# One order of 2764 operations for another, in a four-layer attention kernel: where a stream of matmuls, three busy engines and a few queues set the pace

## The chip, the core and the metric

The kernel runs on one core of a Trainium2 chip. Five engines work side by side, each with its own queue of instructions that it takes strictly in order: TensorE (PE in the profile, with PEld for the loading of its weights), VectorE (DVE), ScalarE (ACT), GpSimd (POOL) and SyncE (SP), which here only starts transfers. Engines wait for each other through semaphores. The metric is the device time of one execution in microseconds.

## The reference

Four residual layers run on one sequence of 2048 tokens with 512 features: a linear-attention block (A), a sliding-window attention block (B), and both once more with the same weights. There are 32 heads of 16 features. Cut to what matters:

```python
def A(x, wqkv, wo):
    q, k, v = heads(x @ wqkv)
    phi = lambda t: jnp.where(t > 0, t + 1, jnp.exp(t)) + 1e-6
    pq, pk = phi(q), phi(k)
    kv, z = einsum("bhsd,bhse->bhde", pk, v), einsum("bhsd->bhd", pk)
    o = einsum("bhqd,bhde->bhqe", pq, kv) / (einsum("bhqd,bhd->bhq", pq, z)[..., None] + 1e-6)
    return merge(o) @ wo

def B(x, wqkv, wo):                       # W = 256
    q, k, v = heads(x @ wqkv)
    scores = einsum("bhqd,bhkd->bhqk", q, k) * 16 ** -0.5
    scores = where((0 <= i - j) & (i - j < W), scores, -1e9)
    return merge(einsum("bhqk,bhkd->bhqd", softmax(scores), v)) @ wo

x = x + A(layernorm(x)); x = x + B(layernorm(x))
x = x + A(layernorm(x)); x = x + B(layernorm(x))
```

## The kernel before

The sequence is cut into 16 tiles of 128 tokens. All four layers are recorded as 2764 operations (a list `s.ops`, built by `graph`), each with the engines that may run it, the buffers it reads and writes, and a function that emits its instructions. Names carry their layer: `1.` is the k and v side of the first linear layer, `2.` its q side and the second layer (the sliding window; `2.b` its projections, `2.a` its attention), `2k.` the k and v side of the third layer, `3.` the q side of the third and the whole fourth (`3.b`, `3.a`). Nothing of layer 3's k side needs more than the tile of its own rows, so layers overlap; but each linear layer's sum over all tokens must be complete before any of its q tiles is used, and this makes a narrow place near 45 us and another near 250 us.

The operations that the text speaks of, by their lines:

- `ln` (lines 814 to 820): mean and variance on DVE, 1/sqrt on POOL (`rs`, line 818), normalised rows `xn` on DVE (line 820). `transp` then turns `xn` into `xT`, either by a DMA transpose that SP starts (line 828) or, for a few tiles, by PE (line 835) and a copy.
- `proj_tok` (line 858): a projection with 128x512 results, four matmuls of 512 columns in two halves; `proj_feat` (line 870): sixteen matmuls of 128 columns. Weights are w_Aq, w_Ak, w_Av, w_Ao for the linear layers and w_Bq, w_Bk, w_Bv, w_Bo for the window layers.
- `phi` (lines 879 to 885): exponential and relu on ACT, the rest on DVE.
- `b_qkv`: two masked copies `kbd` of k per tile (`kb0`, `kb1`, line 971), a copy of q and one of v (line 845). Each of these may run on ACT or on DVE. POOL then starts four transfers that lay v out by heads (`vd`, line 981).
- `b_attn`: scores by four row groups (lines 1007 and 1056, 32 and 16 matmuls in an operation), exponentials on ACT over 128x1024 (lines 1035 and 1077), masks on DVE (lines 1043 and 1095), then the sums over keys with 34-column matmuls (lines 1113 and 1125), the division on DVE and the output projection.

What runs when is not decided when the program is built: a text `ORDER` holds one word for each operation, in order of planned time, and `schedule` walks through it. A word is the operation's number, a mark ' where the second of its possible engines is taken (for the copies the first is ACT, the second DVE), and after a colon the places of its new buffers (PSUM banks, ring slots). Each engine's queue is the words of that engine in this order; `emit` derives the waits from the reads and writes. The text was made beforehand by a planner that is not part of the kernel.

```python
for word in self.plan.split():
    word, _, at = word.partition(":")
    o = self.ops[int(word.rstrip("'"))]
    o.eng, cost = list(o.engs.items())[word.endswith("'")]
```

One more thing depends on the order. Where the half of a `proj_tok` is followed on PE by an operation of another mode, its last matmul is emitted as two, of 448 and 64 columns:

```python
cut = [0, 448, 512] if at[0].cut and kt % 2 else [0, 512]
```

The program also has a slow general path (`general`), taken only when a value is not finite; it isn't executed here.

PE's instructions on the executed path: every matmul is two (its weights, then the multiplication), and a wait that doesn't fit into a matmul is one of its own. Before, they add up to 17,048.

Of the kernel before, what the change touches and what calls it, by code (L numbers as in the profile page):

```python
# [334 lines left out]
230:5.0 194 299 231 184 224:4.0.0 200' 148 207:9 214:7.1 215 300 238:0 271:10 196 195 197 216 208:2.1.3 209 210 180 225 228 284 212 179 278:7.2 279 272:6.2.1  # L335
152 285 286:1 181 301 302:2 314 315 316 169 211 280' 255:11 226 227 229 273 317 213 318:3 256:3.3.2 257 274 239:12 232' 275 25 16 258 259 34 260 23 261 24
262:4.3 263 26 27 246:7.4 240:2.4.0 185 241 247 276 264' 287:13 244 288:5.5.3 201 289 303:14 290 291 310:6.5 311 312' 292 242 248 319:15 294:3.6 277 304:4.7.2
305 308 295 320:5.6.1 306 321 322 324 217 326:2.7 327 243 28 29 17 245 233 249 265 293 307 309 296' 281 297 313 323 328 325 329 330:0 331:1 378:7.4.0 379 380
# [9 lines left out]
658' 671 626 627 672 673 902:6 907:2 684 903 986:0.4.1 987 988 919 449:0 904 955 905:3 881:1 906:3 882:3 883 921:0.6.0 922 923 908 909 685 686:2 687:1 450:5  # L348
884 1407 960:3.0.3 451 961 910:2 911 677:2.1.5 678 912:2 989 962 1408 924 1409 452 474:6.0 475 476 488 477 478:2 479:3 937:3 938 679 933:0.4.1 934 935 674:2.1
675 700 701 1410 932 939 940:1 720 964:0.6.2 702 703 965 966 688:5.0 689 690 691 1411:3 936 942:4 1412:0 941:1 489:0.3 490 943 501 676' 1021:2.6.2 1022 944  # L350
1023 704:0 491 492 493:0 494:1 705:3 967 692:5.2 693 945:2 946 947:0 680 963 721 694' 956:0.2.0 957 958 954 480:4 481 482 644 645 662 1418:7.1 995:0.5.4 996
997 722:1 723:2 1419 1420' 990 913:4 914 915 968:0.2.5 969 970 495:7 496 713:6.2.0 714 715 959 503 497 504:0.0 505 999:4.2.1 1000 1001 972:7 971 977:6 506 973
507 508:3 1056:0.4.0 1057 1058 1024 736 737 974 975:1 738 976:2 978 979 991:0.2.0 992 980:3 981 1421 1422 1423 998 710:7.3 711 712' 993 706:6.1 707 708' 709'
1030:0.4.3 681 716 1031 1032 695:3.1.1 696 994 948:2 1002 1003:0.6.2 697' 1004 949 950 1435 509:3 982:2 510:5 983:4 984 1005 1006 663 1034:0.2.5 1035 985 1036
511 1012:7 512 772 1436 1437 739 1438 740:2 741:4 1060 1007:6 1008 1439:3 1440:2 1424 1449 1450 1091:0.4.1 1092 754 1093 513:3.12.1 514 515 1013 1014 1009
1010:2 1451 517 1011:0 1026:0.4.0 1027 1028 728:2.0 1015:0 1016 1413:3.1.0 1414 1415 729 755 1425:0 1426:1 698 1037 1065:0.6.1 1066 730' 1416 1417 1067
731:5.0.3 732 724:4.2 733 725 1038:0.2.2 1039 1040 1441:7.0.2 1446:6.0 1447 1442 1029 1025 1033 1042:5 1443 1069:0.2.4 1070 1071 726' 1095 1043 727'
1427:4.4.3 1428 1429 699 1452 1448' 1453:1 1041 1047:6 1044 1126:0.2.2 1127 756 1444 1445 1068 746:7.1 747 1017:1 1045:1 1454:5 1046:1 1128 1430 1431 1048
1094 1061:0.4.0 1062 1063 1049 748' 1050:3 1051 757 1052:0 758:2 759:0 1018:3 1019 1100:0.6.3 1101 1102 1020 1465 1466 1467 1460:2.4 773 774 1455:5.3.0 1456
1073:0.3.5 1103 1461 1074 1457 1462 1432:7.3 742:6.3 1433 743 1075 775 1072 1059 1064 1077:2 1078 744 1458 1459 1104:0.4.2 1105 1106 1076 1434' 1079 1082:3  # L360
1083 745' 1080:2 1081:3 516 717 1161:0.6.0 1162 1163 1084 1085:0 764:2.2 765 1086 518 1087:2 766' 1096:0.4.0 1097 1098 1130 749:3.1.2 750 767:2.2.4 776:3 1107
1165 1135:0.6.1 1136 751' 1137 768 769' 1053:5 777:3 1054 1108:0.3.4 1099 1055 1479 760:2.4 761 762' 1468 1109 1110 1111 734 1112:7 1139:0.5.5 1140 1141 1113
1114 763' 1115:1 770 1469:0 1117:4 1118 1116:2 752 1196:0.2.1 519:5.3 1129 520 1197 521 522 1198 523:0 524:3 1119 1120:2 543:7.13.2 544 545 1480 1121 547
1088:1 1199 1131:2.5.0 1142 1089 1090 782:4.3 783 1164 1493 1132 1133 1134 528:7.14.3 1138 1170:0.2.3 1171 784' 1172 529 530 532 778:6.5 779 780' 781' 525:5
526 1143:0.2.2 753 1144 1145 527 790 791 735 1147:4 1148 792 1122:1 1494 1149 1150:0 1146 1151:1 1174:0.6.4 1175 793 1176 794:1 546 1470:3 1476:5.2 1477
1471:3.2.0 1478' 1177 1472 1473 1474 1475 1152:4 1153 1231:0.6.2 1232 1233 1481 531 1482 1154 1155:1 1156 1123:5 533 1124 1166:0.2.0 1125 1507 1173 558:4.15.1
# [3 lines left out]
1484:4 1269 1504:4.6 1505 1204 812:0 1240:0.6.3 1241 1242 1158:2 1159 1502 1506' 1503 1510 1160 1523 1192:3 1524 1193:3 1194 1195 1537 807 1213:0.4.4 1214  # L370
813:2 1217:2 1215 1218 1219 1220:1 1221:2 1244:0.6.5 1245 1246 1485:3.7.1 549:4.3 1212 550 551 1538 552 553:3 554:1 1539 1216 1486 1487 1488 1489 818:2.1 819
820 814:1.1 1235 1236:4.6.0 1237 815 816' 1243 1238 821:0.2.0 822 823 1247 1239 1463:5.4 817 1275:2.6.1 1464 1222:0 1223 1224 1276 1277 1248:2.4.2 1249 1525
# [996 lines left out]
```

## Time and profile before

| what | value |
|---|---|
| time, median of 3 runs | 421.62 us (420.8 to 422.5) |
| time of the profiled execution | 422.47 us |
| span from its first to its last instruction | 421.1 us, granted clock 1.000 |
| PE busy | 392.3 us, 93% of the span |
| ACT busy | 383.6 us, 91% |
| DVE busy | 382.3 us, 91% |
| POOL busy | 106.0 us, 25% |
| moved by DMA | 29.22 MB in 75,720 packets |

The profile counts an engine as busy while an instruction of it runs; the chain that ended last follows, from the last instruction backwards, what released each step. "issue" is time in which an engine waited for nothing that the profile shows. An instruction's mean duration is longer than the step from one to the next, since they overlap in the engine: an exponential of 128x1024 has 1085 ns, and the chain has it six times in 5.50 us.

### The profile page before, as it was taken

What the parts mean: (1) busy time and instruction counts of PE and PEld (TensorE: products, weight loads), DVE (VectorE), ACT (ScalarE), POOL (GpSimd) and SP (SyncE); (2) the same over time, 40 slices, a digit from 0 to 9 for tenths busy, and PEclk for the clock granted to TensorE, in tenths of its full rate; (3) what the DMA queues carried; (4) which work ended last, traced back from release to release, by engine and by line L of the source; (5) the groups of instructions that cost most, each with busy time, mean ns of one, the idle gap of its engine ahead of it and who ended that gap; (6) DMA issues with size and microseconds to landing.
All of it is one profiled execution on the core that took longest, in us unless ns stands there. A gap on an engine that the chain in (4) does not pass through costs nothing.

```text
span 421.1 us, 18887 instructions
## 1 busy us (share of the span) xinstructions
PE 392.3 (93%) x8330; PEld 284.2 (67%) x8404; DVE 382.3 (91%) x1003; ACT 383.6 (91%) x496; POOL 106.0 (25%) x202
## 2 busy tenths in 40 slices
PE   7999989999999899998999999998999899988997
PEld 3655766776766676767586667676767667666675
DVE  7999899999999899998999899999999999978774
ACT  4888679999999999999899767899999999999995
POOL 2230024225232231423131100332322212605200
PEclk9999999999999999999999999999999999999999
DMA  8334426314252130523141201324415422406143
GB/s 265 112 64 138 128 55 126 66 41 99 41 68 43 38 67 16 85 41 59 39 80 22 48 9 39 70 48 68 79 34 80 60 52 33 90 16 117 43 103 92
DMA packets 75720, 29.22 MB, mean 69 GB/s; under 512 B 65264, under 2 KB 73584, under 8 KB 75632
## 3 DMA queue, kind: packets, MB, share of 16 engines
q1 hardware_dynamic: 70336, 22.36, 26.4%
q0 software_dynamic: 4096, 4.46, 5.7%
q8 instruction: 68, 1.11, 1.1%
q10 hardware_dynamic: 1200, 1.11, 0.9%
q14 instruction: 20, 0.16, 0.1%
HBM read 6.29 MB, written 2.10 MB: 20 GB/s over the span
## 4 chain that ended last, share of the span: by engine, by line
PE 42%; ACT 33%; DVE 18%; issue 3%; DMA 3%; POOL 0%; DVEq 0%
ACT pF L1077 23%; PE ps L858 16%; PE ps L870 8%; ACT pH L1035 6%; PE ps L1125 6%; PE ps L1056 5%; PE ps L1113 3%; DVE stats L814 2%; DVE o L954 2%; ACT kbd L971 2%; DMA w_Av<-in_A_wqkv_dram 2%; DVE pF L1095 1%; DVE xres L893 1%; PE ps L916 1%; PE ps L1007 1%
## 5 line engine op out<-in xcount | busy, mean ns | idle before, releaser
L1077 ACT ACTIVATE pF<-ps 128x1024 bf16<-128x1024 f32 x240 | 229.4, 1085 | 4.4 <-PE ps L1056 2.6
L818 POOL TENSOR_TENSOR rstd<-mv,const 128x1 f32<-128x1 f32 x64 | 39.1, 617 | 241.6 <-DVE mv L817 238.6
L981 POOL DMA_DIRECT2D vbd<-vt x128 | 67.1, 532 | 48.2 <-DVE vt L845 30.6
L1035 ACT ACTIVATE pH<-ps 128x1024 bf16<-128x1024 f32 (+1 forms) x64 | 60.3, 1022 | 3.5 <-PE ps L1007 3.2
L1125 PE MATMUL ps<-vbd,pF 128*128 128x34 bf16 x1856 | 60.2, 178 | 2.4 <-issue 2.4
L1125 PEld LDWEIGHTS ps<-vbd,pF 128*128 128x128 bf16 x1856 | 53.3, 96 | 5.5 <-issue 2.7
L1056 PE MATMUL ps<-qT,kbd 32*128 32x128 bf16 x1920 | 48.5, 216 | 5.0 <-ACT pF L1077 2.1
L1095 DVE TENSOR_TENSOR pF<-pF,const 128x512 bf16<-128x512 bf16 (+2 forms) x116 | 46.6, 415 | 3.6 <-ACT pF L1077 3.5
L879 ACT ACTIVATE E<-ps 128x512 bf16<-128x512 f32 x64 | 40.1, 630 | 9.8 <-PE ps L870 6.4
L814 DVE BATCH_NORM_STATS2 stats<-xres 128x6 f32<-128x512 bf16 x64 | 44.0, 689 | 2.0 <-DMA xres<-in_A_x_dram 1.1
L1056 PEld LDWEIGHTS ps<-qT,kbd 32*128 32x128 bf16 x1920 | 28.5, 92 | 22.6 <-ACT pF L1077 9.6
L1043 DVE TENSOR_TENSOR pH<-pH,const 128x1024 bf16<-128x1024 bf16 (+1 forms) x64 | 41.1, 649 | 0.0
L870 PE MATMUL ps<-xT,w_Bq 128*128 128x128 bf16 x512 | 35.5, 219 | 1.0 <-ACT pF L1077 0.7
L870 PE MATMUL ps<-xT,w_Bk 128*128 128x128 bf16 x512 | 35.6, 219 | 0.6 <-ACT pF L1077 0.4
L1113 PEld LDWEIGHTS ps<-vbd,pH 128*128 128x128 bf16 x928 | 29.0, 96 | 8.3 <-issue 2.2
L870 PE MATMUL ps<-xTa,w_Aq 128*128 128x128 bf16 x512 | 34.2, 219 | 0.3 <-DVE pq L883 0.2
L858 PE MATMUL ps<-w_Ak,xTa 128*128 128x512 bf16 (+2 forms) x121 | 32.3, 372 | 1.6 <-issue 0.8
L858 PE MATMUL ps<-w_Av,xTa 128*128 128x512 bf16 (+1 forms) x128 | 32.7, 371 | 1.1 <-issue 0.5
L1113 PE MATMUL ps<-vbd,pH 128*128 128x34 bf16 x928 | 32.7, 178 | 0.9 <-DVE kbd L971 0.3
L858 PE MATMUL ps<-w_Ao,oT 128*128 128x512 bf16 (+2 forms) x119 | 29.4, 354 | 4.2 <-issue 1.6
L870 PEld LDWEIGHTS ps<-xT,w_Bk 128*128 128x128 bf16 x512 | 29.8, 98 | 5.0 <-issue 0.9
L870 PEld LDWEIGHTS ps<-xT,w_Bq 128*128 128x128 bf16 x512 | 29.5, 98 | 5.3 <-issue 2.0
(96 smaller groups left out, 625.6 us busy)
## 6 DMA issues: line engine op xcount, KB each, us to landing
vbd<-vt POOLq DMA_DIRECT2D x128, 34.0 KB, 2.4
xres<-in_A_x_dram SPq DMA_DIRECT2D x16, 128.0 KB, 5.7
out_dram<-xres SPq DMA_DIRECT2D x15, 128.0 KB, 2.3
oT<-o SPq DMA_TRANSPOSE x60, 2.8
w_Ak<-in_A_wqkv_dram ACTq DMA_DIRECT2D x1, 512.0 KB, 5.4
w_Av<-in_A_wqkv_dram ACTq DMA_DIRECT2D x1, 512.0 KB, 6.9
w_Aq<-in_A_wqkv_dram SPq DMA_DIRECT2D x1, 512.0 KB, 7.0
w_Ao<-in_A_wo_dram SPq DMA_DIRECT2D x1, 512.0 KB, 3.9
```

The lines of the kernel that those rows point to most:

```text
L814: s.op(n + ".st", {"DVE": 0.595}, lambda e, en: e.bn_stats(a_st, x.h[:]), reads=[x], writes=[st])
L858: i = e.matmul(g.h[:, a:b], xT.h[:, kt, :], w.h[:, kt, a:b], start=(kt == 0), stop=(kt == 3), skip_group_check=True)
L870: i = e.matmul(g.h[:, f * P:(f + 1) * P], w.h[:, kt, f * P:(f + 1) * P], xT.h[:, kt, :], start=(f == 0 and kt == 0), stop=(kt == 3), skip_ ...
L879: s.op(n + ".e", {"ACT": _act_cost(512)}, lambda e, en: e.activation(E.h[:], g.h, ACT.Exp, bias=0.0), reads=[g], writes=[E])
L981: return [e.dma_start(vbd.h[64 * a:64 * a + 64, j, a], vt.h[64 * j:64 * j + 64, a]) for j in range(2)]
L1035: return e.activation(d, c, ACT.Exp, bias=0.0, scale=DH ** -0.5)
L1043: return e.tensor_tensor(v, v, tr, ALU.mult)
L1056: i = e.matmul(ss[r // 2].h[:, r % 2, k * P:k * P + P], kbds[fj[m] // 2].h[32 * r:32 * r + 32, f, fj[m] % 2, :], qT.h[32 * r:32 * r + 32, ...
L1077: s.op("e%d%d" % (u, g), {"ACT": _act_cost(1024)}, lambda e, en, S=ss[g], pb=pb, g=g: e.activation(pb.h[:, 2 * g:2 * g + 2, :], S.h, ACT.E ...
L1095: return e.tensor_tensor(v, v, tr, ALU.mult)
L1113: i = e.matmul(U.h[:, c:c + 34], pH.h[:, 4 * r + f, 64 * a:64 * a + P], vbds[j // 2].h[:, j % 2, :, 4 * f + r, :], start=first[0], stop=Tr ...
L1125: i = e.matmul(U.h[:, c:c + 34], pFs[at[f, m][0]].h[:, r, at[f, m][1] * P:at[f, m][1] * P + P], vbds[fj[m] // 2].h[:, fj[m] % 2, :, 4 * f ...
```

## The change

Only the text `ORDER` differs: the same 2764 words' numbers in another sequence, with other buffer places and other marks for the second engine. The planner that made it had another rule for when TensorE's instructions are fetched. The first and last lines, and those with the number 60, which is the load of w_Bo (389 is a transpose of o, 597 and 615 are transposes of x, all on SP):

```diff
 ORDER = """
-37 4 0 3 6 7 1 8 9 2 68 61:7 69 70 5 67 71 72:0 73:6.0 62 38 66 85 86 87 10 39 40 88 41 42 43 44 45 46 11 33 12 13 20 47 89:1 22 74 75:7.0.0 76 90:6.1 81:5.0
...
-453:6.9.3 454 457 374:2 375:0 376 427 401 577:0 578:5.0 377 389:3 595 596:1 597:1 610 402 425 611 612 390:7 391 392 628 629 455 579 472 584:0.0 470 580:6.0
-581 582 585 414:4.0 415 613 614:2 615:2 587:7.0.0 588 403:1 404:0 586 583 862:0.2.0 863 864 602:6.1 630 598:1.1 599 426 416 417 471 418:0 419:1 631 632:3
...
-638:7.3 422 894:2.5.1 895 896 664 639 648 641:4.2.2 642 640' 870 898:0.2.2 643' 483:7.10.2 444:5.2 445 665 899 649 650:0 60 666 900 484 487 667 446 447 448:1
...
-2763 2760 2761
+67 6 37 1 4 3 2 0 5 39 7 61:7 8 9 68 69 40 32 70 71 72:0 73:6.0 62 38 66 41 33 74 75:7.0.0 76 42 85 86 87 88 10 11 12 13 43 44 45 46 47 48 49 50 89:1 90:6.1
...
+576 595 457 577:2 470 375:7 376 377 399:2.1 439 442 400 401 596:3 414:0.0 415 610 611 612 613 578:6.0 579 416 402 417 389:3 390:7 391 392 60 614:1 597:1
+580:6.0 455 581 582 583 615:2 403:1 404:1 628 629 630 587:4.0.0 440 441 584:7.0 585 586 456 418:0 419:0 458 631 632:0 588 589 862:2.6.0 598:5.1 863 864 866
...
+2759 2762 2763
 """
```

What it makes of the queues, counted along the built programs:

| | before | after |
|---|---|---|
| operations on PE, ACT, DVE, POOL, SP | 977, 500, 998, 135, 154 | 977, 509, 989, 135, 154 |
| copies of v for the first layer (`1.vc`) on ACT | 10 of 16 | 12 of 16 |
| `2.b.kb` on ACT | 15 of 32 | 17 of 32 |
| `2k.vc` on ACT | 6 of 16 | 8 of 16 |
| `3.b.kb` on ACT | 10 of 32 | 13 of 32 |
| `3.b.vc` on ACT | 3 of 16 | 2 of 16 |
| a last small copy (`3.a.zc`) on ACT | 3 of 4 | 4 of 4 |
| PE's instructions on the executed path | 17,048 | 17,058 |

SP's queue around the load of w_Bo (oT is a transpose of o, xT one of x; the number is the tile):

```
before: oT1 oT2 oT3 xT1 xT2 oT4 oT5 xT3 oT8 oT6 load-w_Bo xT4 xT5
after:  oT1 oT2 oT3 load-w_Bo xT1 xT2 oT4 oT5 xT3 oT6 oT8 xT4 xT5
```

On POOL, the transfers `vd` and the operations `rs` alternate in other groups, in the same number. The order of matmuls on PE differs from the first tens of operations on; each layer's operations stay in about the same part of the span.

More of the change, by code (lines that the diff above doesn't have):

```diff
@@ L348 @@
[L348 to L355, printed above, removed]
@@ new lines @@
+930 931 683 656:7.0 657 658' 928 684 685 902:5 903 907:6 904 905:3 906:3 672 673' 686:1 986:0.2.1 987 988 882:7 687:1 883 721 921:4.0.0 922 923 908 909 884
+1407 910:1 911 450:7 912:3 451 1408 1409 1410 960:2.4.3 961 452 962 924 644 501 677:6.0.5 678 679 722:0 474:0.0 645 475 700 701 702 476 477 478:2 479:2 937:7
+938 503 933:2.4.1 934 935 674:6.1 675 964:0.2.2 965 1411:2 966 1412:0 703 704:3 705:3 932 939 940:2 688:5.0 689 489:0.3 490 690 691 936 942:4 943 676' 941:1
+491 492 493:0 494:0 955 1021:2.6.2 1022 1023 944 945:1 946 692:5.2 693 694' 954 956:0.2.0 957 480:4 481 958 963 482 913:7 967 736 995:0.5.4 996 997 914 915
@@ new lines @@
+1421 1418:4.1 1419 1420' 968:0.2.5 959 1422 495:7 496 497 713:6.2.0 714 969 504:0.0 680 970 971 715 505 506 999:2.4.1 972:7 507 1000 1001 508:3 977:6 1024 973
[3 rows of a table added]
+517 515 1013 1010:1 1014 1037 1015:0 1011:0 1016 716 717 1026:0.2.0 1027 729 740:3 730' 681 1028 741:4 1413:7.0.3 1414 1065:0.4.4 1066 1415 1095 1452 1453:0
+698 731:6.2.3 757 732 724:3.2 725 1067 758:1 726 1446:2.0 1416 1447 1038:0.4.1 1039 1040 1417 733' 1448' 1029 727' 1033 1041 1441:7.1.2 699 1442 1443
+1427:6.5.1 1428 1444 1445 1069:0.2.2 1070 1071 1042:5 1043 1044 1429 1045:2 1047:4 1048 1046:1 1126:0.2.2 746:7.1 747 1127 1128 1430 1431 1017:0 1049 1072
@@ new lines @@
+1893 1894:5.4 1895 1910:0 1911:3 1691 1924 1925 1926 1927 1756 1755 1901:3.2.4 1902 1898:7.0 1899 1757 1903' 1904 1928:1 1905 1829 1704:6 1718:1 1705 1706
+1942 1831 1896 1897 1900 2176:0.4.1 2177 2179 2178 1857:7.14.1 1858 1859 1861 2181:0.2.5 2182 1929:2 1728:4.1 1729 1730 1731 1732:2 1733:0 1912:6.5 1913 1830
+1916:7.1 1917 1918' 1943 1944 1719:1 1720 1721 1960 1961 1914 1915 2213:4.6.3 1962 1945 1946:2 1919:0.1.5 1920 1921' 2183 2184 2214 2215 2200:2.4.2 2201 2202
+1743:6.3 1744 1745 1947:4 1746 2205:2.0.0 2206 2207 1930:5.0 1931 1934:4.2 2180 1747:0 2209:2.6.1 1932' 1933' 1935 1936' 1963 2204 1964:3 1734:1 1735 1736
@@ new lines @@
+1978 2210 2211 1979 2212 2245:2.4.4 2246 2247 1952:0.3 1953 2203 2232:6.2.0 2233 2234 2185:1 1954' 2186 2187 2188:0 2190:5 1937:4.0.1 2191 2192 2208 1938 1939
+2193:2 2189:1 2194 1758:6.1 1759 1760 1761 1762:3 2236 2237:0.2.2 1948:5.1 1922 1949 1950' 1951' 2238 2239 1748:3 1749:4 1965:0 2241:0.6.5 1750 1751 1923
+1970:3.0 1971 2240 2242 2243 1966:2.2 1972 2268:0.4.1 1773:6.3 2235 1774 1940 1941 1980 2216 1775 1776 1981 1777:2 2269 2270 2244 2217:3 2218 2219 2220:0 1967
+2221:0 2248 1763:2 1968 1764:1 1969' 2281:6.4.0 2282 2283 1982:0 1983:1 2253:0 2254 1765 1766 2249:2.6.2 2250 2251 2255 2256:2 2257:3 2271 1973:5.2.0 1974
@@ new lines @@
+1975' 2273:2.0.5 2274 2195:1 1860 2222:4 2223 2224 2225:1 2275 2252 2226 1955:7.1.2 2277:2.5.1 2278 2279 1996 2014 1956 2258:4 1778:0 2259 1957' 2304:0.2.2
+2305 2284 2306 1875 2260 2261:3 1997 1998 2227:3 1988:7.1 1958 2262 1989 2276 2317:0.5.3 2280 2318 2319 1779:4 1990' 1788:2.0 1789 1790 1791 1792:1 1793:2
+1780 1984:7.3 1985 1986 1987 1781 1959 1832 1803:0.2 1804 1805 1999 2000:1 2001:3 2285:2.5.4 2286 1991:4.0.3 2287 1992 1993 1994 2228:7 2229 1806 1807:2
+2309:0.2.2 2310 2311 2272 2289:6 2290 2291 2015 2288 2016 2230 2308 2292:1 2293:0 2313:4.0.5 2314 1808:0 2315 2032 1794:7 1795 1796 2307 2033 2006:6.2
@@ new lines @@
+2340:2.4.0 2341 2342 2312 2007 2008' 2196:7 2197 2198 2353:0.2.1 2354 2355 2343 2017 2018:2 2019:2 2294:6 2295 2296 2321:4.0.0 2322 2323 2009:7.1.4 2297:3
+2263:3 2298 2299:2 2010 2356 2316 2011' 2050 2051 2002:6.4 2003 2004 2005 2034 2345:2.4.4 2346 2347 2320 1818:0.0 1819 1820 1821 1822:1 1809:7 1810 1976 1977
+2325:6 1811 2068 2324 2069 2326 2349:2.0.2 2350 2351 2035 2036:3 2070 2327 2328:2 2027:7.2.5 2028 2329:2 2029' 2376:2.4.1 2377 2378 2348 1877 2300:1 2071
+2072:0 2301 2389:2.6.5 2390 2020:0.5 2302 1833:4.1 1834 1835 2391 1995 2021 2022 2023 1836 2352 1837:3 2330:1 2344 1823:1 2331 1838:0 2332 2037:0 2381:2.6.3
@@ new lines @@
+2382 2383 2333:3 2334 2024:5.3 2025 2361:4 2357:0.2.0 2358 2359 2052 2380 2362 2026' 2053 2054:1 2055:4 1824:5 1825 2073:1 2385:0.6.4 2386 2387 1845 2363 1847
+2379 1826 2364:0 2365:0 2335:2 1839:3 2360 1840 1841 2412:0.4.2 2104 2086 2087 2088 2264:2 2265 2266 2413 2414 2416 1862 2425:6.0.2 2426 2427 2038:3.0 2039
+2040 1848:4.2 1849 1850 1851 1852:1 2366:2 2367 2393:6.0.1 2394 2395 1853:1 2368 2041' 2042:5.0 2417:6.3.0 2418 2419 2043 2044 2369:1 2384 2388 2370 2392
+1863:0.3 1864 2105 1865 1866 1867:3 2012 2013 2397:2 2398 2399 2400:0 1878:6.2 1879 2401:2 2421:0.3.3 1880 2422 2423 1881 2045:5.0.1 1882:1 2046 2047' 1854:2
@@ new lines @@
+2408:7 2409 2410 2569:0.5.1 2523 2510:4 2511 2512 2559 2513:0 2570 2571 2537:0.2.3 2538 2514 2515:0 2539 2161 2162:0 2110:7.4 2540 2111 2112 2113' 2135:6.1.4
+2136 2142 2561:0.4.2 2562 2563 2137' 2564 2132:3.1 2532 2085 2546:2 2547 2133 2134' 2565:0.6.0 2548 2336:5 2549:2 2337 2338 2566 2567 2568 2605:0.3.3 2606
+2541:7 2607 2163:4 2143 2144:3 2145:1 2542 2592:5.0.1 2593 2594 2479:1 2543 2544:1 2545:0 2411 2117:3.0.5 2550 2551:2 2118 2573:4.6.4 2574 2575 2119' 2103
+2577:2 2578 2579 2580:3 2597:0.4.5 2581:3 2572 2598 2199 2599 2128:3.5 2129 2120 2121 2130' 2153:2.2.1 2595 2601:0.6.2 2602 2603 2131' 2154 2146:5.0 2155'
@@ L431 @@
+2147 2628:0.3.2 2629 2630 2148' 2149' 2576 2480:2 2481 2482 2596 2641:6.0.0 2642 2643 2604 2150:5.2 2582:2 2600 2583 2609:3.6.1 2610 2611 2584 2608 2585:0
+2586 2612 2151 2633:0.3.4 2152' 2644 2634 2635 2613:2 2587:1 2614 2615 2616:1 2617:2 2637:6.0.5 2638 2639 2267 2444:5 2445 2446 2171:4.0.2 2664:2.6.0 2665
[7 rows of a table added]
 """
```

72 lines of the change are left out of this document (15 added, 57 removed), and 81 rows, old and new, of the table ORDER.

## The prediction

> **What bounds the kernel now.** I began with the busy shares, then cut the span into stretches, and asked for the chain of waits of each stretch, because an average over four layers hides which engine sets the pace.
>
> ```profile
> PE 392.3 (93%) x8330; PEld 284.2 (67%) x8404; DVE 382.3 (91%) x1003; ACT 383.6 (91%) x496; POOL 106.0 (25%) x202
> PE 42%; ACT 33%; DVE 18%; issue 3%; DMA 3%; POOL 0%; DVEq 0%
> ```
>
> Three engines are within 10 us of each other, so taking work from one and giving it to another helps only where the giver is the late one. The stretches (columns: stretch, its length, then busy us of PE, PEld, DVE, ACT, POOL) say where that is:
>
> ```profile
> 9.00:45.00 36.00, 35.63 (x275) 20.73 (x278) 32.45 (x114) 30.29 (x56) 7.67 (x14) 1.00 0.48 137
> 45.00:60.00 15.00, 13.37 (x172) 10.25 (x171) 14.04 (x44) 11.09 (x19) 1.74 (x4) 1.00 0.19 38
> 60.00:110.00 50.00, 46.76 (x1076) 35.62 (x1090) 47.97 (x127) 48.60 (x63) 18.67 (x34) 1.00 0.41 83
> 110.00:240.00 130.00, 122.59 (x2826) 89.86 (x2844) 121.59 (x304) 123.06 (x151) 32.52 (x58) 1.00 0.28 48
> 240.00:279.00 39.00, 36.48 (x513) 26.54 (x517) 37.02 (x100) 30.45 (x51) 6.62 (x12) 1.00 0.23 44
> 279.00:404.00 125.00, 116.08 (x3065) 87.71 (x3088) 113.39 (x273) 123.87 (x140) 36.46 (x69) 1.00 0.36 63
> 404.00:421.00 17.00, 14.47 (x400) 10.71 (x401) 9.92 (x27) 12.42 (x17) 0.00 (x0) 1.00 0.37 90
> ```
>
> Up to 45 us PE has no gap to speak of (35.63 of 36.00). From 279 to 404 ACT has none (123.87 of 125.00, so 1.1 us idle). Between them no engine is alone; the heads of the chain for three of these stretches settle it:
>
> ```profile
> by line: ACT pF L1077 49.9%; ACT pH L1035 19.9%; ACT kbd L971 9.4%; DMA xT<-xn 8.8%; PE ps L870 3.1%; PE ps L858 2.5%; ACT qT L845 2.0%; ACT vt L845 2.0%; ACT E L879 2.0%; ACT pq L882 2.0%; PE ps L1007 1.6%; PE ps L1056 1.5%; issue 1.3%; PE
> by line: PE ps L858 24.3%; PE ps L870 15.6%; PE ps L1125 13.3%; PE ps L1056 8.4%; PE ps L1113 6.6%; issue 4.7%; DVE pF L1095 3.3%; DVE pH L1043 2.3%; ACT pF L1077 2.2%; DVE stats L814 2.2%; PE ps L1007 1.9%; POOL rstd L818 1.6%; DVE o L1137
> by line: DVE o L954 11.0%; DVE stats L814 10.6%; DVE xres L893 7.8%; DVE kvacc L1316 7.6%; DVE kbd L971 7.0%; DVE pq L883 6.6%; DVE E L880 6.1%; DVE pk L885 5.4%; DVE dn L953 4.9%; DVE xn L820 4.1%; issue 3.7%; PE ps L858 3.4%; PE ps L870 3
> ```
>
> In order: 60 to 110 is ACT's, 110 to 240 is PE's with 4.7% "issue", 240 to 279 is DVE's.
>
> **Part 1, the fetch of PE's instructions.** The stall that such a rule can be about shows as "issue" inside a run of matmuls that waits for nobody. These rows are the instruction queue's packets, the waits of line 1125 on "issue", three pieces of the chain, and PE's timeline around the first:
>
> ```profile
> q8 instruction: 68, 1.11, 1.1%
> PE ps L1125 <- issue: 2.4, 4, 0.8
> 117.92 0.60 issue
> 140.42 0.77 issue
> 151.20 0.68 issue
> 114.05 0.40 PE L1056 MATMUL ps<-qT,kbd 32*128 32x128 bf16 x16
> 114.38 0.61 PE L858 MATMUL ps<-w_Ao,oT 128*128 128x512 bf16 x2
> 114.87 0.96 PE L1113 MATMUL ps<-vbd,pH 128*128 128x34 bf16 x32
> 115.67 0.56 PE L1125 MATMUL ps<-vbd,pF 128*128 128x34 bf16 x16
> 116.16 0.41 PE L1007 MATMUL ps<-qT,kbd 32*128 32x64 bf16 x32
> 116.51 1.07 PE L870 MATMUL ps<-xTa,w_Aq 128*128 128x128 bf16 x16
> 117.41 0.51 PE L1125 MATMUL ps<-vbd,pF 128*128 128x34 bf16 x14
> 118.52 1.02 PE L1125 MATMUL ps<-vbd,pF 128*128 128x34 bf16 x34 [0.60 <-issue]
> ```
>
> The queue brought 1.11 MB in 68 packets, 16.3 KB each, and PE's path has 17,048 instructions (each matmul counts twice, once for its weights, and a separate wait once), about 17,073/67 = 255 per packet. Counting along the built program, the four pauses of line 1125 stand at instructions 3519, 4543, 5054 and 10431: apart by 1024, 511 and 5377, that is by 4, 2 and 21 times 256 within one. So they are page ends. Three lie on the chain, 0.60 + 0.77 + 0.68 = 2.05 us; that is all the change can win here.
>
> Starts in the timeline give the pace of a page: 16 matmuls of line 1056 in 0.33 us (21 ns), 32 of line 1113 in 0.80 (25), 32 of line 1007 in 0.35 (11), 16 of line 870 in 0.90 (56). The page shown takes 3.6 us. By the same pace the pages ahead of the other two pauses on the chain hold 2.7 us (79 matmuls of 34 columns, 16 and 32 of scores) and 2.9 us. Page plus pause is 3.5, 3.5 and, for the one shown, 4.2; pages of 3.3 to 3.7 also run without a pause. In the changed order I count, by the same pace, the shortest pages: 3.2, 3.2, 3.3, 3.4, 3.4, 3.5, 3.5. The two worst are gone, but more are just short. Against 3.5 the first five lack 0.3 + 0.3 + 0.2 + 0.1 + 0.1 = 1.0 us; one of them stands at the place of the page shown, and if it needs 4.2 again the rest is 1.7. So 0.35 to 1.05 of the 2.05 is won: **-0.7**. Ends: -2.05 with no pause left, and if all five take 4.2, 21.0 - 16.5 = 4.5 of pauses, +2.4.
>
> [...]
>
> **Part 2, work moved between engines.** The order also decides which of two engines makes some copies: nine that DVE made are now ACT's. What one costs:
>
> ```profile
> 65.61 1.16 ACT kbd L971 x2
> 145.27 1.21 DVE vt L845 x2
> ```
>
> 0.58 us on ACT, 0.60 on DVE, by stretch:
>
> - Up to the first exponential (60 us): ACT has three more, DVE two fewer. PE sets this stretch; ACT sat idle 5.7 us from 9 to 45 and takes 1.7 unseen: **0**. Without that cover, +0.6 (one copy late at the start); if DVE's relief counts, -1.2.
> - 60 to 110: the three extra ACT copies lie ahead of it and none is added inside: 0.
> - 110 to 240: ACT gets about two more, DVE two fewer, while PE sets the pace. ACT is busy 123.06 of 130, so I take a quarter of 1.16: **+0.3**; ends -1.2 and +1.2.
> - 240 to 279: DVE's stretch. Its queue between the second layer's last exponential and the fourth layer's first is shorter by about one copy: **-0.6**; ends 0 and -1.8 (three copies).
> - 279 to 404: three masked copies of k (line 971) go from DVE to ACT, 3 x 0.58 = 1.7 on the engine with 1.1 us of idle in 125. **+1.5**; ends +0.6 (all the idle closes) and +1.7. This is the dearest term: what DVE gains here (113.39 of 125) was not late.
>
> **Part 3, the queues.** SP now issues the load of w_Bo after its third transpose of o and ahead of its first two transposes of x for the second layer; before, it stood seven transposes later.
>
> ```profile
> 51.67 1.19 SPq L828 DMA_TRANSPOSE oT<-o  x1
> 56.26 4.38 DMA xT<-xn
> w_Bo<-in_B_wo_dram SPq DMA_DIRECT2D x1, 512.0 KB, 4.3
> xT<-xn SPq DMA_TRANSPOSE x30, 2.7
> ```
>
> The load would go out at 51.67 + 1.19 = 52.9 and land at 57.2, while the transpose that the chain takes is issued at 56.26: 0.9 us overlap. It blocks nothing by waiting, as it waits for nothing; it shares engines. I take half the overlap, **+0.5**; ends 0 (landed before) and +4.3 (the transpose goes through behind all of it).
>
> POOL's queue is reordered too: each transfer of v waits there with the next 1/sqrt(variance) behind it.
>
> ```profile
> POOL vbd L981 <- DVE vt L845: 30.6, 9, 8.4
> DVE xn L820 <- POOL rstd L818: 2.2, 4, 0.7
> ```
>
> POOL stands for up to 8.4 us in such a wait, yet DVE lost only 2.2 us to a late rstd: **0**, cover being DVE's other tiles; without it, another +2.2.
>
> **Part 4, split matmuls.** The last matmul of a half is cut into 448 + 64 columns where another kind follows; PE's path grows by 10 instructions, five matmuls.
>
> ```profile
> L858 PE MATMUL ps<-w_Bv,xT 128*128 128x64 bf16 x20 | 3.9, 193 | 0.0
> ```
>
> At 193 ns, mostly overlapped: **+0.1**, ends 0 and +1.0. The clock is 1.00 in every stretch and stays.
>
> **Sum.** -0.7 + 0 + 0.3 - 0.6 + 1.5 + 0.5 + 0.1 = +1.1 us. The profiled execution took 422.47 (span 421.1 and 1.4 around it), which gives 423.6; it lay 0.85 above the median of the timed runs, 421.62, so the median becomes **422.7**.
>
> **The rivals.**
>
> *w_Bo in front of the transposes (slower).* Place: SP, 53 to 60 us. The chain's 4.38 us for that transpose against a usual 2.7 shows that transfers crowd here even without a load. If it waits for the whole load, the 0.5 becomes 4.3: 421.62 + 0.6 + 4.3 = **426.5**. It decides once the transpose lands over 2 us late, since ACT's stretch from 60 on is 48.60 of 50 and cannot catch up. Against it: by the issue times the load is nearly through.
>
> *The pauses stay (the change doesn't do what it says).* The shortened list of pages above trades two bad ones for several small; if nothing is won the sum is +1.8, **423.4**. [...]
>
> *All pauses go and DVE's relief counts (faster).* -2.05 - 1.8 + 0.3 + 0.6 = -2.95: **418.7**. For it: the chain of 240 to 279 is DVE nearly throughout. Against it: ACT's 125 us stretch must then start nearly 3 us earlier.
>
> *New idle in ACT's long stretch (slower).* Only 1.1 us of idle exists there, so a new order can hardly better it and may lose; at twice the present idle with the ends of the other terms, about **425**.
>
> **How the numbers follow.** Sum as worked out 0.34; pauses stay 0.15; w_Bo 0.15; new idle 0.06; faster 0.30. A measurement of this kernel tells about 0.5%, 2.1 us, from no change: 419.5 to 423.7 is "same". The sum's own case (420.7 to 424.7) gives 0.03 faster, 0.23 same, 0.08 slower; the pauses 0.08 same, 0.07 slower; w_Bo 0.01 and 0.14; new idle 0.06 slower; the faster case 0.27 and 0.03 same. Together 0.30, 0.35, 0.35. The ends of all terms reach from 416.0 to 435, but not at once; leaving 1 in 10 out on each side, from the faster case less one copy-pair to the w_Bo case plus a new pause: 417.4 to 427.6.
>
> **What would show it.** In the new profile: pauses on "issue" at line 1125 adding to 1.0 to 1.7 us, none over 0.7 (part 1); ACT from the first to the last exponential of the fourth layer longer by 1.5 us and still 98% busy (part 2); the first DMA transpose of x landing within 5 us of its issue (part 3). Wrong it would be if the long stretch starts over 2 us away from 279, or if PE's own share between 110 and 240 changes by more than 1 us.

## The result, and the profile after

The changed kernel took 423.84 us (median of 12 runs, 422.88 to 425.66), the kernel before 422.06 us in the same set (420.80 to 423.15): ratio 1.0046, 95% interval 1.003 to 1.0062, so 1.8 us slower. The prediction had 1.1 us slower and a range of 417.4 to 427.6. The profiled execution took 423.65 us with a span of 422.3; the one before 422.47 and 421.1, so the two profiles are 1.2 us apart.

The page of the changed kernel: busy shares, then the chain of waits by engine.

```profile
PE 393.2 (93%) x8330; PEld 285.3 (68%) x8409; DVE 378.2 (90%) x994; ACT 387.3 (92%) x505; POOL 105.9 (25%) x202
ACT 45%; PE 33%; DVE 17%; issue 3%; DMA 1%; POOL 0%; SPq 0%; DVEq 0%; POOLq 0%
```

DVE lost 4.1 us of work and ACT gained 3.7, and the chain went the same way: ACT holds 45% of it (33% before), PE 33% (42% before). "issue" holds 3% as before, so the pauses were not reduced. The stretches (columns as in the prediction; the last three figures are the granted clock, the share of the DMA engines and GB/s):

```profile
110.00:240.00 130.00, 124.35 (x2861) 91.97 (x2887) 119.64 (x302) 124.61 (x156) 34.30 (x62) 1.00 0.29 51
279.00:404.00 125.00, 115.80 (x3029) 86.72 (x3056) 112.39 (x273) 124.15 (x141) 35.59 (x67) 1.00 0.36 62
404.00:422.00 18.00, 15.11 (x456) 11.95 (x443) 10.23 (x27) 13.15 (x18) 0.00 (x0) 0.99 0.28 84
```

PE still sets the pace from 110 to 240 (124.35 of 130, 122.59 before) and ACT is still full from 279 to 404. To find where the time went, three marks serve: the exponential (line 879) of the last tile of the third layer's k side, the first exponential of the fourth layer (line 1035), and that of its last tile. Their rows on ACT's timeline, before and then after:

```profile
248.00 0.60 ACT L879 ACTIVATE E<-ps 128x512 bf16<-128x512 f32 x1 [0.27 <-PE ps L858]
267.22 1.08 ACT L1035 ACTIVATE pH<-ps 128x512 bf16<-128x512 f32 x2 [0.50 <-PE ps L1007]
403.90 2.14 ACT L1035 ACTIVATE pH<-ps 128x1024 bf16<-128x1024 f32 x2
```

```profile
248.33 0.60 ACT L879 ACTIVATE E<-ps 128x512 bf16<-128x512 f32 x1 [0.23 <-PE ps L858]
266.59 1.08 ACT L1035 ACTIVATE pH<-ps 128x512 bf16<-128x512 f32 x2 [0.52 <-PE ps L1007]
404.28 1.28 ACT L1035 ACTIVATE pH<-ps 128x1024 bf16<-128x1024 f32 x1
```

| stretch, us | before | after | difference |
|---|---|---|---|
| start to the first mark | 248.00 | 248.33 | +0.33 |
| to the fourth layer's first exponential | 19.22 | 18.26 | -0.96 |
| to the last tile's first exponential | 136.68 | 137.69 | +1.01 |
| to the last instruction | 17.16 | 18.04 | +0.88 |
| sum | 421.06 | 422.32 | +1.26 |

So the narrow place near 250 us became faster, ACT's long stretch slower by the same amount, and the loss that remains stands at the two ends: ahead of 248, and behind 404. Behind 404 the chain of the changed kernel reads:

```profile
409.40 0.34 PE ps L1056 x16
409.73 0.06 PE ps L1063 x11
409.80 0.67 issue
410.47 0.20 PE ps L1063 x5
```

PE stops for 0.67 us in the middle of 16 equal matmuls. Counted along the built program, this is a page end: it stands a multiple of 256 instructions, within one, behind the pauses at 106.92 and 380.87. It lies on the chain where the last tile's matmuls set the pace, and the time was not given back behind it: this stretch is 0.88 us longer.

### The profile page after: what moved, and what is told of

Read it like the earlier page. It is cut to its first block, busy times and chain, and to the rows that moved or that the text cites. A ratio compares the mean times of both kernels' runs of the same rounds, so it can differ in the third digit from the quotient of the medians.

```text
span 422.3 us, 18893 instructions
## 1 busy us (share of the span) xinstructions
PE 393.2 (93%) x8330; PEld 285.3 (68%) x8409; DVE 378.2 (90%) x994; ACT 387.3 (92%) x505; POOL 105.9 (25%) x202
## 4 chain that ended last, share of the span: by engine, by line
ACT 45%; PE 33%; DVE 17%; issue 3%; DMA 1%; POOL 0%; SPq 0%; DVEq 0%; POOLq 0%
ACT pF L1077 32%; PE ps L858 13%; ACT pH L1035 9%; PE ps L870 5%; PE ps L1125 5%; PE ps L1056 4%; DVE stats L814 3%; ACT kbd L971 3%; PE ps L1113 2%; DVE o L954 2%; DMA xres<-in_A_x_dram 1%; DVE xres L893 1%; PE ps L916 1%; DVE xn L820 1%; DVE pq L883 1%
## 5 line engine op out<-in xcount | busy, mean ns | idle before, releaser
L870 PE MATMUL ps<-xT,w_Bk 128*128 128x128 bf16 x512 | 34.6, 219 | 0.1
L870 PEld LDWEIGHTS ps<-xTa,w_Aq 128*128 128x128 bf16 x512 | 29.9, 98 | 5.7 <-DVE pq L883 2.0
L858 PE MATMUL ps<-w_Bo,oT 128*128 128x512 bf16 (+2 forms) x124 | 29.1, 346 | 3.7 <-issue 1.7
```

What stands on the lines that cost most here:

```text
L858: i = e.matmul(g.h[:, a:b], xT.h[:, kt, :], w.h[:, kt, a:b], start=(kt == 0), stop=(kt == 3), skip_group_check=True)
L870: i = e.matmul(g.h[:, f * P:(f + 1) * P], w.h[:, kt, f * P:(f + 1) * P], xT.h[:, kt, :], start=(f == 0 and kt == 0), stop=(kt == 3), skip_ ...
```

## The experiments

All kernels were timed beside the kernel before in their set (its medians there: 421.94 to 422.51 us), and all ratios are to it. Edited programs have their line numbers shifted by 2 or 4 (line 1125 is 1127 or 1129).

**Four kernels that move only the page ends.** The general path is not executed, but its instructions lie in memory ahead of the fast path. Waits put into it (two share one instruction) shift every page end of PE, and not one executed instruction changes. Counted along the built programs, all 17 pauses of over 0.5 us on "issue" that lie on the chain of the two kernels, of the six shifts of this section and of the run with the load moved stand at the same remainder of 256 within one, once the shift is added: they are page ends, and the shifts move them.

```diff
                 gen.put(gen.order)
+                for _ in range(200):
+                    s.handle["PE"].wait_ge(done.sem, done.val)
```

This is the shift by 100 instructions; the others have 448, 152 and 440 waits. Each run is read from one profiled execution, while the times of a kernel spread over 2.1 to 3.6 us; the profiled executions of the shifts by 224 and by 220 were the longest of their twelve (425.35 and 425.98 us). The expectations call a page short when it lasts under 3.75 us without its pauses. The 3.75 is my choice, and no run shows a limit there: the longest pause of the changed kernel ended a page of 4.3 us (106.92 - 102.62).

> The changed order, word for word, with 100 PE instructions more in the general path, which is not executed but lies in memory ahead of the fast path. Nothing that runs is changed; only the places where the 256-instruction pages of PE end move by 100 instructions. By the changed kernel's trace (pauses taken out) no page of this phase is shorter than 3.75 us, against 3.4 to 3.6 us of pauses on issue in the changed kernel. Theory (the loss comes in part from pauses that the page ends make, one of them at 410 us where PE sets the end): the pauses on issue of 0.4 us and more are nearly gone (under 1 us in sum), the page end at 410.47 makes no pause any more, and the time falls by 0.7 to 2 us, to 421.8 to 423.1; ratio to the kernel before 0.999 to 1.003. Rival (page ends cost nothing, the whole loss is work moved onto ACT): the time stays at 423.8, ratio 1.0046.

Measured: 422.01 us, ratio 0.9993 (0.9979 to 1.0008). Within the interval the whole loss of the change is gone, by moving page ends alone. The expected end of the tail's pause came true; "under 1 us in sum" did not quite, as a pause of 0.84 us appeared at 295.13 in a page that is not short, beside one of 0.47 at 19.70 that is no page end.

> The changed order with 224 PE instructions more in the general path, which is not executed: the phase of the page ends that the changed kernel's trace shows as the worst, with pages of 3.0, 3.2, 2.9, 3.1 and 3.0 us (3.5 us short of 3.75 in sum), the last of them at 407 us. Theory: pauses of 0.5 to 1.2 us at 107, 131, 142, 175 and 410 us, more than 4 us in sum; those of the middle are given back in part, the one of the tail is not; time 424.3 to 426, ratio 1.006 to 1.010. Rival (page ends cost nothing): 423.8, ratio 1.0046.

Measured: 423.55 us, ratio 1.0029 (1.0012 to 1.0047). Worse than the shift by 100, but not worse than the change itself, and below the expected 1.006: of the five short pages one ended in a pause of 0.75 us and two in pauses of 0.45 and 0.28. The list of short pages told the direction, not the amount.

> The order of before, word for word, with 76 PE instructions more in the general path, which is not executed: of all phases of the page ends the one with the least short pages in the trace of before (0.14 us short of 3.75 in sum, against pauses of 2.7 us in sum at the phase of before). Theory: the pauses at 118.5, 141.2 and 151.9 us go; as ACT's stretch after 279 has only 1.1 us idle, and the pauses of the middle lie on the chain, 0.5 to 2 us are won: 420.0 to 421.5, ratio 0.995 to 0.999. Rival (page ends cost nothing, or all of it is given back before the end): ratio 0.999 to 1.001.

Measured: 422.57 us, ratio 1.0001 (0.9985 to 1.0018): nothing won. The three pauses that were to go went, though a new one of 0.89 us came at 116.96. ACT's last tile was earlier (402.89 against 403.90 before), then the gain went at the very end. SP's last store, before and in the shift by 76:

```profile
419.28 0.33 SPq L1209 DMA_DIRECT2D out_dram<-xres  x1
```

```profile
418.33 1.74 SPq L1211 DMA_DIRECT2D out_dram<-xres  x1
```

Its issue took 1.74 us instead of 0.33. The DMA queues of the shift by 76 from 417.9 to 419.7 (share of the engines for a queue; KB each and us to landing for an issue):

```profile
q8 instruction: 1, 0.02, 5.9%
...
out_dram<-xres SPq DMA_DIRECT2D x1, 64.0 KB, 2.8
out_dram<-xres ACTq DMA_DIRECT2D x1, 64.0 KB, 3.0
```

A packet of PE's instructions runs beside the two last stores, which land after 2.8 and 3.0 us; in the kernel before they took 1.5 and 1.6, with no such packet in that time. The last page end lay just ahead of PE's last instruction, so one more page was fetched at the worst moment.

> The order of before with 220 PE instructions more in the general path, which is not executed: its worst phase, pages of 3.05, 3.4, 3.0, 3.7, 3.5 and, at 407 us, 2.9 us. Theory: the place of the page ends alone, with the order of before, makes the loss that the changed kernel shows: a pause of 0.7 us or more near 410 us that nothing hides, and others in the middle; time 422.8 to 424.5, ratio 1.002 to 1.006. Rival (page ends cost nothing): ratio 0.999 to 1.001.

Measured: 423.23 us, ratio 1.0031 (1.0017 to 1.0046). With the order of before, a poor place of the page ends alone makes two thirds of the loss that the change shows. The pause of the tail stands where it was expected, a little shorter than the expected 0.7:

```profile
413.63 0.52 PE L1127 MATMUL ps<-vbd,pF 128*128 128x34 bf16 x14 [0.64 <-issue]
```

A longer pause, of 1.67 us at 298.56, was not on the list of short pages. The granted clock behind it was 0.54 from 299 to 301 us and 0.74 from 301 to 304.

**A second phase, and two edits under it.** A phase is one place of the page ends. The shift by 20 puts the last page end behind PE's last instruction.

> The changed order, word for word, with 20 PE instructions more in the unexecuted general path. At this phase the trace of the changed kernel (pauses taken out) has one page under 3.75 us (3.72 at 148 us), the pages of the tail last 4.06, 3.83 and 3.85 us, and the last page end lies behind PE's last instruction, so no page is fetched while the last rows are stored. Theory (a page end costs where its page is short, and most of all in the tail; the order itself is worth nothing against before): as good as the shift by 100 or better, ratio 0.996 to 1.000, and no pause over 0.4 us after 404 us. Rival (the shift by 100 was better for another reason than its page ends, or any shift does it): ratio as the changed kernel's, 1.003 to 1.006.

Measured: 421.91 us, ratio 1.0001 (0.9980 to 1.0022); its times reach from 420.96 to 424.13, so the median lies lower than the ratio suggests. At a second phase, too, the changed order shows no loss beyond the interval. Its three marks on ACT:

```profile
246.95 0.60 ACT L881 ACTIVATE E<-ps 128x512 bf16<-128x512 f32 x1 [0.23 <-PE ps L860]
265.21 0.60 ACT L1037 ACTIVATE pH<-ps 128x512 bf16<-128x512 f32 x1 [0.52 <-PE ps L1009]
403.07 1.28 ACT L1037 ACTIVATE pH<-ps 128x1024 bf16<-128x1024 f32 x1
```

PE at the place where the changed kernel stopped for 0.67 us: the small matmuls of line 1065 run through, and the projection follows after 0.16 us.

```profile
409.69 0.25 PE L1065 MATMUL ps<-const 32*128 32x32 bf16 x8
410.10 0.81 PE L860 MATMUL ps<-w_Bo,oT 128*128 128x512 bf16 x4 [0.16 <-issue]
```

> As the run before it (changed order, shift by 20), but the twelve copies of the fourth layer's q, k and v whose engine the change exchanged stand on the engine that they had before: ACT has three masked copies of k fewer in its long stretch. Theory (these three copies lengthen ACT's stretch from 279 to 404 by about 1 us, and the end with it): the time from the first to the last tile's first exponential of the fourth layer falls from about 137.7 to 136.7 us and the ratio lies 0.002 to 0.0035 below that of the run before it. Rival (DVE, with twelve other copies back in places planned without them, is late in turn, or the stretch isn't what sets the end): no difference, or slower by 0.001 to 0.003.

The words that differ, pulled together:

```diff
-1903' 1918' 1914 1915 1972 1969' 1993 2023 2040 2041' 2112 2137'
+1903 1918 1914' 1915' 1972' 1969 1993' 2023' 2040' 2041 2112' 2137
```

Measured: 436.61 us, ratio 1.0344 (1.0312 to 1.0376). Far worse than either theory had it. The chain ahead of the loss, and three stretches of 4 us around it (the last figures of a row are the granted clock, the share of the DMA engines and GB/s):

```profile
271.49 0.70 DVE xres L897
...
272.22 0.71 DVE stats L818
...
273.13 1.29 DVE kbd L975 x2
...
274.57 0.43 PE ps L1060 x16
```

```profile
272.00:276.00 4.00, 1.38 (x21) 0.67 (x21) 2.75 (x8) 1.11 (x3) 0.65 (x1) 1.00 0.01 1
276.00:280.00 4.00, 3.28 (x54) 2.76 (x55) 2.69 (x6) 3.68 (x6) 2.09 (x4) 0.55 0.31 68
280.00:284.00 4.00, 3.78 (x53) 2.58 (x51) 2.97 (x6) 2.13 (x3) 0.00 (x0) 0.59 0.39 37
```

Two copies of k stand in DVE's queue behind a residual and a layer norm, where the order had not planned them; PE waits 3.1 us for DVE, and then has 0.55 to 0.59 of its clock for about 8 us. That is one of three places: of the 12.7 us between the two profiled spans, 2.0 are lost by the fourth layer's first exponential (267.18 against 265.21), about 5 here, and about 5 between 329 and 358 us, where PE waits 1.93 us for DVE at 331.01 and the clock falls to 0.83 from 330 to 340. So exchanging marks in place tells nothing of the price of a copy.

> As the first run of this set (changed order, shift by 20), but the load of w_Bo stands on SP seven transposes later, where it was before. Theory (by the trace of the changed kernel the first transposes of x for the second layer land as early as before, so the load ahead of them costs nothing): the second layer's first exponential starts within 0.3 us of 60.8, and the ratio is that of the first run within 0.0015. Rival (the prediction's 0.5 us for the load): the second layer's exponentials start 0.5 us or more earlier, and 0.001 or more of the ratio is won.

Measured: 423.18 us, ratio 1.0013 (0.9994 to 1.0032). The second layer's first exponential came at 60.79, in the shift by 20 at 60.80: the load's place costs nothing there, as the theory has it. What it lost against the shift by 20 in its profile, 2.6 us at the eighth tile's first exponential (119.64 against 117.01), begins with a pause at a page end that the shift by 20 did not have (last section).

> The order of before with 28 PE instructions more in the unexecuted general path. In the shift by 76 the last exponentials came about 1 us earlier than before, but the fetch of one more page at 417.95 stood beside the last store, whose issue took 1.74 us (0.33 before); here the last page end lies behind PE's last instruction and the pages of the tail last 4.01, 4.08 and 4.46 us. One page of 3.12 us at 147 us stays. Theory (page ends and the fetch beside the last store are all that the shift by 76 lost): the store is issued in under 0.6 us, and the time is 0.3 to 1.5 us less than before, ratio 0.9965 to 0.9995. Rival (the 1.74 us was chance, and page ends of this order are given back): ratio 0.999 to 1.001.

Measured: 422.92 us, ratio 1.0013 (0.9996 to 1.0030). The last store was issued in 0.33 us with no packet beside it, as expected, yet nothing was won: pauses of 0.89, 0.66 and 1.17 us came at 118.92, 141.62 and 152.74, where the list of short pages had only the third.

**Joining the two orders, and the copies again.** The next kernel takes the first 1852 words of the changed order and the other 912 operations in the order of before, with before's places for the buffers (renumbered in the rings where they differed).

> The changed order for the first 1852 words (up to the start of the second tile's exponentials in the fourth layer, about 273 us), then the order of before for the other 912, with 20 PE instructions more in the unexecuted general path. By the shift by 20, the changed order without costly page ends reaches that point at 272.14 (before: 273.64); by the shift by 28, the order of before needs 130.25 us from there to the last tile's first exponential, the changed order 130.93. Page ends of both parts lie where their traces show no short page and no pause in the tail. Theory (the early part of the changed order is better by about 1 us, its late part worse by 0.7 us because of the copies on ACT, and page ends hid the first): the last tile's first exponential at 402.4, the last instruction about 419.6, profiled time about 421.0, ratio 0.9955 to 0.9985, under before and under the changed order. Rival (parts don't add: what the early part wins is given back where the two orders meet, or new page ends make new pauses): ratio 0.999 to 1.003.

Measured: 426.32 us, ratio 1.0090 (1.0061 to 1.0118): the rival. From 269 to 277 us the chain is almost only DVE's queue, PE waits 2.3 us, and the clock falls again:

```profile
277.33 0.61 PE L1060 MATMUL ps<-qT,kbd 32*128 32x128 bf16 x16 [2.34 <-DVE o L958]
```

The granted clock from 276 to 280 is 0.58. A pause of 1.2 us at 107.9 came on top, so the ratio is not the price of the join alone.

> The order of before with one edit: three masked copies of k of the fourth layer (tiles at 28.86, 29.86 and 33.86 of the planner's time, one each) run on ACT instead of DVE, each at its own place in the order; PE's program keeps its length. Theory (the prediction's term: ACT is the late engine from 279 to 404, so three copies of 0.58 us cost 0.6 to 1.7 us there, and the end moves with them): from the first to the last tile's first exponential of the fourth layer 137.3 to 138.4 us (before 136.68), ratio 1.001 to 1.004. Rival (ACT waits anyway where the copies fall, or what DVE gains pays for it): 136.7 us or less, ratio 0.999 to 1.001.

The words that differ:

```diff
-2023' 2040' 2112'
+2023 2040 2112
```

Measured: 424.21 us, ratio 1.0042 (1.0026 to 1.0059). The two marks of the stretch, on ACT:

```profile
267.35 0.60 ACT L1037 ACTIVATE pH<-ps 128x512 bf16<-128x512 f32 x1 [0.50 <-PE ps L1009]
405.52 1.22 ACT L1037 ACTIVATE pH<-ps 128x1024 bf16<-128x1024 f32 x1
```

405.52 - 267.35 = 138.17 us against 136.68: the stretch is 1.49 us longer for three copies. In the order of before, the price is what the theory says: one kernel at one place of its page ends, which the edit does not move.

> The changed order with 20 PE instructions more in the unexecuted general path, as in the shift by 20, and three masked copies of k of the fourth layer (the same three as in the run that gave them to ACT) on DVE as before: two at their places, one three words later, behind the DVE operation that it follows closest. Theory (these copies cost ACT's long stretch 1.0 to 1.5 us, page ends the rest): from the first to the last tile's first exponential of the fourth layer 136.4 to 136.9 us instead of 137.86, ratio 0.9965 to 0.9990, under the kernel before. Rival (in this order DVE has no room, and PE waits for the copies as it did where twelve copies were exchanged): the stretch stays at 137.9 us or more, ratio 1.000 or above. A pause at 107.9 us, which two of four kernels with this page phase had and two had not, would add up to 1.3 us on either theory.

The lines of the order, cut to what matters:

```diff
-2022 2023 1836 2352 1837:3 2330:1
+2022 1836 2352 1837:3 2023' 2330:1
...
-2040 2112
+2040' 2112'
```

Measured: 423.20 us, ratio 1.0030 (1.0018 to 1.0042): the rival. The stretch grew to 404.82 - 265.52 = 139.30 us from 137.86. Pieces of the chain at the first copy that was given back:

```profile
320.92 0.58 ACT kbd L975
...
321.52 0.75 DVE kbd L975
322.27 0.60 DVE pH L1047
...
323.55 0.60 DVE pH L1047
324.15 0.60 DVE qT L849
```

In the shift by 20 this piece is ACT's (two copies, then three exponentials without a gap). Here the copy pushes DVE's masks back. PE waits 0.48 us for a mask at 323.01, and ACT, which waits for nothing between 318 and 350 in the shift by 20, waits five times for PE, 2.1 us in all.

> As the run before it, with 100 PE instructions more instead of 20: the second phase of the page ends with no short page in the tail. Theory: from the first to the last tile's first exponential 136.7 to 137.2 us instead of 138.12 (a pause at 295 us stays in it), ratio 0.9960 to 0.9985. Rival: 138.1 us or more, ratio 0.9993 or above.

Measured: 424.91 us, ratio 1.0072 (1.0047 to 1.0097). The same failure at the second phase: 406.31 - 265.75 = 140.56 us, where the shift by 100 has 138.12. No version that I ran beats the kernel before by more than its interval; the shifts by 100 and by 20 are level with it.

## Why the prediction was right, and why its sum was not

The sum was near (+1.1 us forecast, +1.8 measured, +1.2 between the profiles), but its steps were wrong by as much, in opposite directions; that the time came out near is luck. Of the signs that the prediction named, the transpose of x landed 2.4 us after its issue, the long stretch began within 2 us of its old start, and ACT was 99% busy in it, as forecast; the stretch grew by 1.0 us instead of 1.5. PE's own share between 110 and 240 rose by 1.76 us, to 124.35, over the 1 us that was to mean "wrong"; 35 more matmul records lie in that window. The same stretches with the page ends moved show the steps:

| stretch, us | before | before, shift 76 | after | after, shift 20 |
|---|---|---|---|---|
| start to the first mark | 248.00 | 246.86 | 248.33 | 246.95 |
| to the fourth layer's first exponential | 19.22 | 19.19 | 18.26 | 18.26 |
| to the last tile's first exponential | 136.68 | 136.84 | 137.69 | 137.86 |
| to the last instruction | 17.16 | 18.62 | 18.04 | 17.34 |
| sum | 421.06 | 421.51 | 422.32 | 420.41 |

Each column is one execution, so differences of some tenths are not told from chance here.

**Part 1, "0.35 to 1.05 of the 2.05 is won: -0.7": this step failed, with the wrong sign.** At their phase the page ends cost the changed order 1.4 us up to 248 us and 0.7 in the tail, against the shift by 20, and 1.8 to 1.9 us between the medians (423.84 against 422.01 and 421.91, from different sets; by the ratios 2.2 and 1.9). The page ends of before cost 1.1 us up to 248 us, and the two other places tried for a gain win nothing in the medians. Two things were wrong in the working. (Its 17,073 instructions should be the 17,048 named beside it, 254 to a packet, which changes nothing.) It ranked pages by length and asked 3.5 us of each; but the longest pause of the changed kernel, at 108.09, ended a page that ran from 102.62 and lasted 4.3 us without it, longer than any on my list:

```profile
104.17 0.41 PE L1056 MATMUL ps<-qT,kbd 32*128 32x128 bf16 x16 [0.29 <-ACT pF L1077]
104.51 0.97 PE L1113 MATMUL ps<-vbd,pH 128*128 128x34 bf16 x32
105.33 0.56 PE L1125 MATMUL ps<-vbd,pF 128*128 128x34 bf16 x16
105.84 0.41 PE L1007 MATMUL ps<-qT,kbd 32*128 32x64 bf16 x32
106.19 0.73 PE L1125 MATMUL ps<-vbd,pF 128*128 128x34 bf16 x22
108.09 0.81 PE L1125 MATMUL ps<-vbd,pF 128*128 128x34 bf16 x26 [1.17 <-issue]
```

This pause goes with a late fetch: the packet of PE's instructions ran from 105.61 to 106.67, about 3 us after the page began, while for the median page of this kernel it starts under 1 us after. PE went on 1.42 us after the packet's end. So it is with the others: of the 17 pauses named above, 16 end 1.28 to 1.55 us after the end of such a packet, and one 1.87. These pages paused where they were short against the start of their fetch, and the working had only the length. And it priced all pauses alike, while the one behind 404 us was not given back (18.04 us from there to the end, against 17.34 without it). The rival "the pauses stay" was the better reading of this part, and its 423.4 lies nearer the measured 423.84 than the sum's 422.7. The expected sign, pauses of line 1125 adding to 1.0 to 1.7 with none over 0.7, is refuted by the 1.17 alone.

**Part 2, the narrow place, -0.6.** The start of the fourth layer moved by -0.63, from 267.22 to 266.59, and the stretch itself by -0.96 at either phase: right in place and sign, 0.4 too small.

**Part 2, three copies of k, +1.5.** The price was right for the order in which I worked it out: the same number of copies, moved alone in the order of before, cost 1.49 us. In the changed order ACT's stretch is 1.0 longer, at either phase. It is not shown that this is the copies' doing: taken back there, three copies made it 1.4 us longer still. An order is laid around its engines, and the price of a move belongs to the order it is made in.

**Part 2, the middle, +0.3.** The two orders without their early pauses reach 248 us within 0.1 us of each other. The +0.33 measured there is page ends, so the agreement is accidental.

**Part 3, w_Bo, +0.5.** Nothing: moving the load back left the first exponential of the second layer where it was. The rival that lets the transpose wait for the whole load is refuted. POOL's reordering left no wait on the chain: its share there is 0% in both kernels.

**Part 4, +0.1.** Not measured apart. PE's busy time rose by 0.9 us, which holds more than the split matmuls. "The clock is 1.00 in every stretch and stays" held in the profiled execution (0.999) but not in all: in seven of the twelve timed runs of the changed kernel the mean granted clock was 0.992 or 0.996, with a median of 424.20 us, and in the other five it was 0.999 or 1.000, with 423.35. All twelve runs of the shift by 100 had 1.000, and the kernel before never less than 0.999 in the 91 runs timed beside the edits. So part of the 1.8 us is lost clock, which the sum put at nothing, and it went when the page ends were moved by 100.

Together: without its costly page ends the changed order stands at 0.9993 and 1.0001 of before, where the terms beside part 1 had given +1.8 us. Within these intervals the whole measured loss is the place of the page ends, with the clock that falls behind some of their pauses. That the change "has another rule for when instructions are fetched" does not show as shorter waits: where it won, at the narrow place, it won by the order.

## What to carry to other kernels

Where PE runs long trains of short matmuls, shift its program by some tens of unexecuted instructions before comparing two orders: here that alone was worth 0.5%, as much as the whole change. Look for a page end in the tail first, because a pause there was not given back here (18.04 us from 404 to the end with it, 17.34 without), and see that no page is fetched beside the last store (1.74 us to issue, 0.33 without). And price a move between engines in the order in which it is to run: an exchange of twelve marks in place cost 3.4%, with copies behind the wrong work in a queue.

## What was not expected of the hardware

**When a page is fetched varies between runs.** The shift by 20 and the kernel with the load moved back have the same PE program with the same page ends, and PE's timelines agree within 0.03 us up to 106.2. In the shift by 20 the DMA queues show one packet of PE's instructions between 103.2 and 104.9:

```profile
q8 instruction: 1, 0.02, 3.4%
```

In the other kernel nothing at all moves between 103.2 and 104.9:

```profile
DMA packets 0, 0.00 MB, mean 0 GB/s; under 512 B 0, under 2 KB 0, under 8 KB 0
```

Its packet comes between 105.1 and 106.6, and PE pauses:

```profile
106.25 0.47 PE L1129 MATMUL ps<-vbd,pF 128*128 128x34 bf16 x12
107.95 1.07 PE L1129 MATMUL ps<-vbd,pF 128*128 128x34 bf16 x36 [1.23 <-issue]
```

The shift by 20 ran through this place. So a page end that paused for 1.23 us in one run made no pause in another with the same program of PE, and it was not crowding on the DMA engines here. In the changed kernel the fetch for the pause at 108.09 came late as well (105.61), behind PE's wait of 0.29 us for ACT at 104.17; but the pair above has that wait in both kernels, so it decides nothing by itself. What starts a fetch is open, and no run was made for it.

**PE's clock halved behind some short pauses, and not behind others.** After the pause of 1.23 us above the granted clock fell; after the one of 1.17 us at the same place in the changed kernel it did not. The same stretch in the one and in the other:

```profile
110.00:112.00 2.00, 1.78 (x18) 1.32 (x20) 1.56 (x4) 1.35 (x2) 0.00 (x0) 0.50 0.32 66
```

```profile
110.00:112.00 2.00, 1.95 (x34) 1.26 (x33) 2.00 (x5) 2.00 (x3) 0.00 (x0) 1.00 0.32 66
```

The former was 2.6 us late at the eighth tile, the latter 1.25 (118.26 against 117.01). In the shift by 224 a pause of 0.75 us at 411.41 was followed by a clock of 0.52 from 413 to 416, while in the shift by 28 one of 1.17 us that ended at 152.74 was not followed by any fall (1.00 from 153 to 158). In the 4 us from 104 to 108, which hold the two pauses at the one place, PE was busy for 2.53 us where the clock fell and for 2.75 where it did not; in the shift by 28 it was busy for 1.77 of the 3 us from 150 to 153. Why the clock falls behind one such pause and not behind another is open.

**A store issued beside a fetch of instructions took longer to issue:** 1.74 us instead of 0.33, shown above, and not only there. The 14 profiles hold 238 stores of results. Of these, 26 took over 0.65 us to issue, up to 2.34, and every one of them ends 0.28 to 0.40 us after the end of a packet of PE's instructions that ran beside it. No store without such a packet took over 0.62 us. In the kernel before, the store issued at 414.94 took 1.10 us, and the packet beside it ran from 414.72 to 415.65. Four stores that began during a packet, over 0.3 us before its end, were issued in 0.33 to 0.37 us all the same. Why is open, and the effect was seen, not varied by itself.
